# Loads around a layer border taken in contiguous quarters, and w_o loaded one head at a time

## The chip, the cores and the metric

The kernel runs on one core of a Trainium2 chip. The core has TensorE (PE in the profile; its weight loads are listed as PEld), VectorE (DVE), ScalarE (ACT), GpSimd (POOL) and SyncE (SP). In this kernel SP does nothing but issue the loads, which 16 DMA engines carry out. The metric is the time of one execution on the device in microseconds (us). The median of three executions before the change is 650.86 us (650.15 to 652.39).

## The reference

Four tokens (one for each of B = 4 sequences) pass through attention, feed-forward, attention, feed-forward; both attention steps use the same caches and weights, and so do both feed-forward steps.

```python
def _A_ref(x, k_cache, v_cache, wq, wo):      # x [4, 1, 512]; caches [4, 8, 8192, 128], bf16
    q = (x @ wq).reshape(B, Sq, 32, 128).transpose(0, 2, 1, 3)
    k = jnp.repeat(k_cache, 4, axis=1)        # 8 kv heads serve 32 query heads
    v = jnp.repeat(v_cache, 4, axis=1)
    p = softmax(einsum("bhqd,bhkd->bhqk", q, k) * 128 ** -0.5)
    return einsum("bhqk,bhkd->bhqd", p, v).transpose(0, 2, 1, 3).reshape(B, Sq, 4096) @ wo
def _B_ref(x, w_gate, w_up, w_down):          # [512, 1792], [512, 1792], [1792, 512]
    return (silu(x @ w_gate) * (x @ w_up)) @ w_down
x = A_x
for _ in range(2):
    x = x + _A_ref(_layernorm(x), A_k_cache, A_v_cache, A_wq, A_wo)
    x = x + _B_ref(_layernorm(x), B_w_gate, B_w_up, B_w_down)
```

A pair of sequence and kv head has 8192 keys of 128 numbers, 2 MB, and as many values. The 32 pairs make 134 MB a layer.

## The kernel before

**Units and rooms.** One pair of kv head g and sequence b is a *unit* u = 4g + b. Its keys are one load of 2 MB (K u), its values another (V u). SBUF has 8 *slots* of 2 MB for them (`NSLOT`), each spoken of in 8 blocks (`NB`), named `s{slot}.{block}`. Layer 0 takes the units in the order 0 to 31, layer 1 in the order 29, 30, 31, 0 to 28. The keys and values of units 29 to 31 stay in slots 0 to 5 from layer 0 to layer 1 (`NKEEP`), so that layer 1 loads 29 units. At a layer's end w_gate, w_up and w_down lie in slots 6 and 7 (`at_w` gives the blocks of each); w_q, w_o and three quarters of w_up stay in SBUF for good.

**The list of loads.** `items` is one list, in the order in which SP issues: K0, K1, V0, K2, V1, ..., then w_gate, w_up, w_down, and the same for layer 1. `pump` walks it: the slot of the next item is fixed (`home`), and the walk stops where that slot isn't free. `finished` frees a slot once the last scores (K) or products (V) that read it are in the program, and `T.dma` lets SP wait for exactly those. All loads go through SP's one queue in list order. A key or value load is cut by `runs` so that its source is read in rows of 32 KB. The last values of each layer (`split`) are four loads instead, each with 4 KB of every partition. w_o is eight loads of 512 KB (4 KB in a partition), put in pairs behind the 3rd, 5th, 7th and 9th key or value load.

**Around the border.** After the last products of layer 0 come the projection by w_o, layernorm, and `ffn(False)`: w_gate and w_up matmuls, the SiLU on DVE and ACT, w_down in three pieces (`WD`). All of slots 6 and 7 is given free behind the last w_down matmul; K0 and K1 of layer 1 go there. The slot of K29 goes to V0 and that of K30 to K2, by halves (`half`), the first half when four of the eight blocks have been scored. The other slots go on as they are finished.

**The work of a unit.** DVE turns each of the 8 key blocks (`turn`, one 128x512 transpose in place), PE multiplies it (`scores`); then follow maximum, exponentials and the turned probabilities (`max_p` to `total`, kept in `line` and let out between the blocks by `advance`), and `values`: PE multiplies the values, ACT and DVE add up (`own_first`, `own_others`), `add_rows` and `scale_o` write the unit's four heads into `oT`. When four units of a kv head are done, `out_proj` puts `oT` into another order by 16 small matmuls and a copy (`o4`) and multiplies by w_o. PE, DVE and ACT each run their instructions in order. Units 29 to 31 are already turned when layer 1 begins.

**Projection by w_q in layer 1.** The four heads of unit 29's kv head are projected first (`qproj([first])`); the other 28 heads are one lump of 112 matmuls in front of K0's blocks.

**Loops.** `roll` looks for units whose instructions repeat every four units and plays them as a loop on PE, DVE and ACT, each by itself; what lies outside is written out. It starts at the first unit with the longest repeat.

The lines that carry the layer border:

```python
        halves = {("K", 1, unit_order[1][k]): items[ends[0] + 3 + k] for k in range(2)}      # 330
        split = {items[e - 3] for e in ends}                                                 # 328
                      writes=places + ["wg"])                                                # 360
            free.update((NKEEP, NKEEP + 1))                                                  # 731, end of ffn
            pump()
```

Of the kernel before, what the change touches and what calls it, by code (L numbers as in the profile page):

```python
# [8 lines left out]
BF16 = mybir.dt.bfloat16  # L9
# [136 lines left out]
def bass_interleave_layers__gqa_block_cached__swiglu_ffn__decode_kernel(  # L146
# [44 lines left out]
    with ExitStack() as es:  # L191
# [16 lines left out]
        wd_sb = kvf[:, f1:f1 + FO * D].rearrange("p (f n) -> p f n", f=FO)  # L208
        places = [f"s{s}.{q}" for s in range(NKEEP, NSLOT) for q in range(NB)]
        room = lambda a, b: places[(a - f0) // (TB * Dh):(b - 1 - f0) // (TB * Dh) + 1]  # L210
        at_w = {"wg": room(f0, f0 + KT * F) + ["wg"], "wu": room(f0 + KT * F, f1) + ["wu", "wu3"],
                "wd": room(f1, f1 + FO * D)}
        WD = ((0, 6), (6, 12), (12, 14))
        wq_sb = sb("wq_sb", [P, KT, HqDh], BF16)

        wo_sb = sb("wo_sb", [P, G, REP, D], BF16)
        wo_b = wo_sb[:].rearrange("p g e n -> p (g e n)").bitcast(U8)
# [8 lines left out]
        o4 = sb("o4", [P, REP, B], BF16)  # L226
# [40 lines left out]
        sem_h = [[sem(f"sem_h{k}{i}") for i in range(2)] for k in range(2)]  # L267
# [57 lines left out]
        for n, it in ((3, ("wo", 0)), (6, ("wo", 1)), (9, ("wo", 2)), (12, ("wo", 3))):  # L325
            items.insert(n, it)
# [3 lines left out]
        halves = {("K", 1, unit_order[1][k]): items[ends[0] + 3 + k] for k in range(2)}  # L330
# [14 lines left out]
        def runs(src):  # L345

            n = src.shape[0] * src.shape[1] * 2
            return src.rearrange("(r k) n -> r (k n)", r=32 * -(-n // (32 * RUN)))

        def load_weight(name, i=0):  # L350
            if name == "wq":
                T.dma("sp", [(wq_sb[:, i, :], runs(A_wq[i * P:(i + 1) * P, :]))], sem_w["wq"][i], writes=[f"wq{i}"])
            elif name == "wo":
                n = G // 4
                w = REP * Dh
                T.dma("sp", [(wo_sb[:, g, :, :].rearrange("p e n -> p (e n)"), runs(A_wo[g * w:(g + 1) * w, :]))
                             for g in range(i * n, (i + 1) * n)], sem_w["wo"][i], writes=[f"wo{i}"])
# [15 lines left out]
        def pump():  # L373
            while issued[0] < len(items):
# [19 lines left out]
                src = cache[b, g, :, :].rearrange("(p t) d -> p (t d)", p=P)  # L394
                if it in split:
                    w = TT * Dh // NQ
                    n8 = NB // NQ
                    for q in range(NQ):
                        T.dma("sp", [(kv[:, s, q * w:(q + 1) * w], src[:, q * w:(q + 1) * w])], sem_l[q],
                              writes=[f"s{s}.{q * n8 + k}" for k in range(n8)])  # L400
                else:
                    T.dma("sp", [(kv[:, s, :], runs(cache[b, g, :, :]))], sem_s[s], writes=[f"s{s}.{q}" for q in range(NB)])
                issued[0] += 1

        def half(it, i):
            to = halves[it]
            kind, L, u = to
            s = slot_of[it]
            if i == 0:
                assert items[issued[0]] == to  # L410
                slot_of[to] = s
                issued[0] += 1
            w = SL // 2
            src = (A_k_cache if kind == "K" else A_v_cache)[u % B, u // B, :, :].rearrange("(p t) d -> p (t d)", p=P)
            T.dma("sp", [(kv[:, s, i * w:(i + 1) * w], src[:, i * w:(i + 1) * w])], sem_h[unit_order[1].index(it[2])][i],
                  writes=[f"s{s}.{i * NB // 2 + k}" for k in range(NB // 2)])

        def finished(it):
# [5 lines left out]
            elif it in halves:  # L424
                half(it, 1)
                pump()
            else:
                free.add(slot_of[it])
                pump()
# [97 lines left out]
        def keys(L, u):  # L527
            def block(q):
# [9 lines left out]
                if q == NB // 2 - 1 and ("K", L, u) in halves:  # L538
                    half(("K", L, u), 0)
# [4 lines left out]

            for q in range(NB):
                if (L, u, q) not in turned:
                    turn(L, u, q)
# [3 lines left out]
        def values(L, u):  # L551
            g, b = unit_gb(u)
            bk = OBK[turn_of[u]]
            def begin():
# [33 lines left out]
            def add_rows():  # L588
                T.pe(bank(LNB)[:, 0:REP], acc[:], head[:], reads=["acc", "head"], writes=[f"pb{LNB}"],
                     start=True, stop=True)  # L590
                scale_o(LNB)
# [16 lines left out]
            def scale_o(k):  # L608
                T.op("dve", lambda e: e.tensor_tensor(oT[:, g // (G - 1), :, b], bank(k)[:, 0:REP], rl[:, rl_of[u], :],
                                                      ALU.mult),  # L610
                     reads=[f"pb{k}", f"rl{rl_of[u]}"], writes=[f"oT{g // (G - 1)}"])
# [7 lines left out]
            done.add((L, u))  # L619
            if all((L, g * B + k) in done for k in range(B)):  # L620
# [10 lines left out]
        def out_proj(g):  # L631

            pick = ident.rearrange("p (j e) -> p e j", e=REP)
            ob = bank(OUTB)[:, XB:2 * XB].rearrange("p (e b) -> p e b", b=B)
            for c in range(REP):
                for h in range(REP):
                    T.pe(ob[h * QB:(h + 1) * QB, c, :], pick[:, c, :], oT[:, g // (G - 1), h, :],
                         reads=[f"oT{g // (G - 1)}", "ident"], writes=[f"pb{OUTB}"], sig=(h == REP - 1),
                         start=True, stop=True)
            T.op("dve", lambda e: e.tensor_copy(o4[:], ob),  # L640
                 reads=[f"pb{OUTB}"] + [f"wo{i}" for i in range(4)], writes=["o4"])
            for nt in range(KT):
                for c in range(REP):
                    T.pe(bank(OUTB)[:, nt * B:(nt + 1) * B], ((c, nt), wo_at(c * D + nt * P)), o4[:, c, :], at=g,
                         reads=["o4"], writes=[f"pb{OUTB}"], sig=(c == REP - 1), start=(c == 0), stop=(c == REP - 1))
# [212 lines left out]
```

## Time and profile before

| what | value |
|---|---|
| the profiled execution: its time, its span | 651.29 us, 649.3 us |
| busy share of the span: PE, DVE, ACT, POOL | 78%, 69%, 18%, 3% |
| moved by DMA | 274.27 MB, mean 422 GB/s |
| share of 16 DMA engines' span, loads alone | 98.7% |
| mean TensorE clock granted | 0.855 of full |
| issues: K and V whole, w_o, last V in quarters | 118 of 2 MB, 8 of 512 KB, 8 of 512 KB |

The profile is one execution. Its time exceeds its span by 2.0 us, which lies outside the first and the last instruction, and it is 0.43 us longer than the median of the three shown. In the windows below, "DMA share" is the mean busy share of the 16 DMA engines, and it counts a packet where it starts, so that it can pass 1 in a short window. The GB/s beside it are the bytes of those packets. Busy time alone doesn't show what a stage waits for; the time from a load's issue to its landing and the rate of the DMA engines are read together with it.

### The profile page before, as it was taken

How to read it: one execution, taken by the hardware profiler on the slowest of the kernel's cores; microseconds unless marked ns; L12 is line 12 of the kernel's file. 1: busy time of each engine (PE TensorE's matmuls, PEld its weight loads, DVE VectorE, ACT ScalarE, POOL GpSimd, SP SyncE). 2: the span in 40 equal slices, each digit the busy share in tenths (PEclk: the TensorE clock that was granted, in tenths of full speed). 3: DMA queues.
4: the chain of work that ended last, by engine and by line, in shares of the span. 5: the costliest groups of instructions: out<-in, count | busy, mean ns of one | idle time of the engine just before them, and what ended most of it. 6: DMA issues, size and time to landing. Idle time of an engine off the chain costs nothing.

```text
span 649.3 us, 12407 instructions
## 1 busy us (share of the span) xinstructions
PE 505.3 (78%) x4896; PEld 324.7 (50%) x4896; DVE 446.2 (69%) x1079; ACT 116.3 (18%) x391; POOL 19.3 (3%) x73
## 2 busy tenths in 40 slices
PE   1657788878868787886877986898888787886886
PEld 1534454545435454553556654555555454553556
DVE  2556676776866767776762386979797777686683
ACT  0021111211211212221220211213131221121120
POOL 0000000000000000000000000000000000000000
PEclk9998787797987879789795978979897969799795
DMA  8999999999999999999999999999999999999996
GB/s 347 427 431 428 433 429 434 428 440 428 432 436 424 444 426 432 439 424 442 428 416 361 421 408 430 417 439 430 432 438 424 438 430 436 436 424 438 430 415 279
DMA packets 13085, 274.27 MB, mean 422 GB/s; under 512 B 2712, under 2 KB 2720, under 8 KB 3744
## 3 DMA queue, kind: packets, MB, share of 16 engines
q1 hardware_dynamic: 13056, 273.89, 98.7%
q8 instruction: 17, 0.28, 0.2%
q14 instruction: 12, 0.10, 0.0%
HBM read 273.88 MB, written 0.00 MB: 422 GB/s over the span
## 4 chain that ended last, share of the span: by engine, by line
DMA 50%; DVE 24%; PE 21%; issue 3%; SPq 1%; ACT 1%; DVEq 0%; POOL 0%; ACTq 0%; POOLq 0%
DMA kvf<-in_A_k_cache_dram 47%; PE ps L99 21%; DVE kvf L117 15%; DVE acc L117 4%; DMA kvf<-in_B_w_up_dram 3%; DVE one L117 1%; DVE pT L117 1%; SPq L135 1%; DVE m L117 1%; DVE scr L117 1%; ACT pb L117 0%; ACT acc L117 0%; DVE oT L117 0%; DVEq L782 0%; SPq L133 0%
## 5 line engine op out<-in xcount | busy, mean ns | idle before, releaser
L117 DVE STREAM_TRANSPOSE kvf<-kvf 128x512 f32<-128x512 f32 x488 | 322.3, 686 | 68.6 <-DMA kvf<-in_A_k_cache_dram 68.6
L99 PE MATMUL ps<-kvf,zq 128*128 128x256 bf16 x2048 | 332.6, 305 | 21.7 <-DVE kvf L117 16.4
L99 PEld LDWEIGHTS ps<-kvf,zq 128*128 128x128 bf16 x2048 | 202.6, 111 | 92.7 <-DVE kvf L117 40.2
L117 ACT ACTIVATE pb<-m 1x128 f32<-1x128 f32 x64 | 19.7, 308 | 441.1 <-DVE m L117 441.1
L99 PE MATMUL ps<-kvf,pT 128*16 128x512 bf16 x960 | 68.0, 407 | 1.4 <-DVE rl L117 1.4
L117 DVE SCALAR_TENSOR_TENSOR acc<-ps,own,acc 128x128 f32<-128x128 f32 x180 | 63.2, 351 | 6.5 <-ACT acc L117 1.9
L99 PE MATMUL ps<-identf,one 128*1 128x128 f32 x64 | 17.9, 279 | 43.2 <-DVE one L117 43.2
L117 DVE TENSOR_REDUCE one<-ps 128x1 f32<-128x256 f32 x64 | 25.9, 405 | 37.0 <-PE ps L99 36.5
L99 PEld LDWEIGHTS ps<-identf,one 128*1 128x1 f32 x64 | 5.1, 80 | 73.6 <-DVE one L117 67.5
L99 PE MATMUL ps<-head,acc 128*128 128x4 f32 x120 | 24.5, 275 | 21.4 <-DVE acc L117 21.3
L99 PEld LDWEIGHTS ps<-head,acc 128*128 128x128 f32 x120 | 20.5, 214 | 37.0 <-DVE acc L117 36.7
L117 ACT ACTIVATE pb<-ps,one,rstd 128x256 bf16<-128x256 f32 x64 | 36.1, 563 | 2.1
L467 POOL TENSOR_TENSOR zq<-scr,quad 128x64 bf16<-128x64 bf16 x62 | 18.1, 293 | 604.0 <-PE ps L99 564.9
L99 PEld LDWEIGHTS ps<-kvf,pT 128*16 128x16 bf16 x960 | 19.1, 91 | 33.8 <-issue 21.9
L99 PE MATMUL ps<-one,pb 1*128 1x1 f32 x128 | 26.2, 272 | 11.5 <-ACT pb L117 11.2
L99 PEld LDWEIGHTS ps<-one,pb 1*128 1x128 f32 x128 | 20.8, 202 | 28.8 <-ACT pb L117 26.0
L99 PE MATMUL ps<-o,wo_sb 128*128 128x4 bf16 x256 | 26.5, 166 | 9.1 <-DVE o L117 9.1
L117 DVE STREAM_TRANSPOSE pT<-pb 128x256 bf16<-128x256 bf16 x64 | 26.1, 408 | 9.7 <-ACT pb L117 9.7
L99 PEld LDWEIGHTS ps<-rsm,one 128*128 128x128 f32 x128 | 23.9, 232 | 12.2 <-ACT rsm L117 10.4
L99 PEld LDWEIGHTS ps<-o,wo_sb 128*128 (+1 forms) x256 | 22.8, 103 | 12.8 <-issue 9.0
L99 PE MATMUL ps<-rsm,one 128*128 128x4 f32 x128 | 21.7, 240 | 9.0 <-ACT rsm L117 9.0
L117 DVE TENSOR_TENSOR xT<-xT,ps 128x16 f32<-128x16 f32 x21 | 3.6, 172 | 33.1 <-PE ps L99 33.1
(61 smaller groups left out, 197.1 us busy)
## 6 DMA issues: line engine op xcount, KB each, us to landing
kvf<-in_A_k_cache_dram SPq DMA_DIRECT2D x60, 2048.0 KB, 28.8
kvf<-in_A_v_cache_dram SPq DMA_DIRECT2D x58, 2048.0 KB, 31.2
wq_sb<-in_A_wq_dram SPq DMA_DIRECT2D x4, 1024.0 KB, 8.4
wo_sb<-in_A_wo_dram SPq DMA_DIRECT2D x8, 512.0 KB, 37.7
kvf<-in_A_v_cache_dram SPq DMA_DIRECT2D x8, 512.0 KB, 14.7
kvf<-in_B_w_gate_dram SPq DMA_DIRECT2D x8, 448.0 KB, 16.8
kvf<-in_B_w_down_dram SPq DMA_DIRECT2D x14, 256.0 KB, 17.6
kvf<-in_B_w_up_dram SPq DMA_DIRECT2D x5, 448.0 KB, 18.0
```

Of the source, the lines that this page charges most:

```text
L99: return e.matmul(out, lhsT=lhsT if at is None else lhsT(place(at)), rhs=rhs, **kw)
L117: self.tape[engname].append((repr((name, args, kw)), lambda e, _: getattr(e, name)(*args, **kw), left, sig, None))
L135: ins = e.add_instruction(mybir.InstDMACopy(name=self.nc.get_next_instruction_name(), mode="Copy", queue="qSPDynamicHW", ins=e.lower_ap_dm ...
L467: T.op(eng, lambda e: e.tensor_tensor(dst, q4, m4_, ALU.mult), reads=keys_ + ["quad"], writes=["zq"])
```

## The change

- **w_o** is loaded one head at a time: 32 loads of 128 KB in place of 8 of 512 KB. The 128 rows of w_o of a head go one to a partition (1 KB each); the source is read in 16 rows of 8 KB. They stand in threes behind every key or value load from the third on, so that the last two come behind V5. With the head's own rows in the partitions, `out_proj` multiplies `oT` by w_o at once: the 16 ordering matmuls and the copy are gone. The wait for w_o moves from that copy to `scale_o` of the unit that completes a kv head.
- **Slots 6 and 7 given up in parts.** Three quarters of K0 (layer 1) are issued behind the w_gate matmuls, the fourth behind the w_up matmuls; half of K1 behind the first piece of w_down, which is now 8 of 14 blocks, the rest behind the last.
- **Quarters for halves.** V0 and K2 take the slots of K29 and K30 by quarters, after 2, 4, 6 and 8 scored blocks. Every quarter, also of the last values of a layer, is 512 KB that lie together in memory, read in rows of 16 KB and written as 4 KB a partition. The units concerned (the last of each layer; 0, 1, 2 in layer 1) have this order of keys in K and V.
- **Order at the head of layer 1.** DVE turns K0 while K30 is scored and K1 while K31 is scored. V31 is multiplied in front of K0, not behind it, and in front of V31 come the 28 heads of w_q, four at a time. V3's load changes places with K4's.
- **Small things.** `add_rows` uses other columns of its PSUM bank; `roll` takes the latest start among those with the same number of turns.

```diff
+        WD = ((0, 8), (8, 12), (12, 14))
...
-                "wd": room(f1, f1 + FO * D)}
-        WD = ((0, 6), (6, 12), (12, 14))
+                **{f"wd{j}": room(f1 + a * D, f1 + b * D) + [f"wd{j}"] for j, (a, b) in enumerate(WD)}}
...
-        for n, it in ((3, ("wo", 0)), (6, ("wo", 1)), (9, ("wo", 2)), (12, ("wo", 3))):
-            items.insert(n, it)
+        for h in range(Hq):
+            items.insert(3 + h // 3 * 4 + h % 3, ("wo", h))
+        i, j = (items.index((k, 1, unit_order[1][2 * NRES + n])) for k, n in (("K", 1), ("V", 0)))
+        items[i], items[j] = items[j], items[i]
...
+        heirs = {("K", 1, unit_order[1][k]): items[ends[0] + 3 + k] for k in range(2)}
+        fours = {(L, unit_order[L][-1]) for L in range(2)} | {(1, u) for u in unit_order[1][NRES:2 * NRES]}
...
+                T.dma("sp", [(wo_sb[:, i, :], runs(A_wo[i * Dh:(i + 1) * Dh, :], 16))], sem_w["wo"][i // G],
+                      writes=[f"wo{i}"])
...
+        def part(it, s, a, b, sem_):
+            kind, L, u = it
+            assert (L, u) in fours
+            n = NB // NQ
+            w, m = n * TB * Dh, S // NQ
+            src = (A_k_cache if kind == "K" else A_v_cache)[u % B, u // B, :, :]
+            T.dma("sp", [(kv[:, s, q * w:(q + 1) * w], runs(src[q * m:(q + 1) * m, :])) for q in range(a // n, b // n)],
+                  sem_, writes=[f"s{s}.{k}" for k in range(a, b)])
+
+        def place(it, s):
+            assert items[issued[0]] == it
+            slot_of[it] = s
+            issued[0] += 1
+
+        def quarter(it, i):
+            to = heirs[it]
             if i == 0:
+                place(to, slot_of[it])
+            n = NB // NQ
+            part(to, slot_of[it], i * n, (i + 1) * n, sem_h[unit_order[1].index(it[2])][i])
...
-                if q == NB // 2 - 1 and ("K", L, u) in halves:
-                    half(("K", L, u), 0)
+                if ("K", L, u) in heirs and (q + 1) % (NB // NQ) == 0 and q < NB - 1:
+                    quarter(("K", L, u), q // (NB // NQ))
...
+            i = unit_order[L].index(u)
+            ahead = unit_order[1][i + 2] if L == 1 and i in (1, 2) else u
             for q in range(NB):
-                if (L, u, q) not in turned:
-                    turn(L, u, q)
+                if (L, ahead, q) not in turned:
+                    turn(L, ahead, q)
...
-                     reads=[f"pb{k}", f"rl{rl_of[u]}"], writes=[f"oT{g // (G - 1)}"])
+                     reads=[f"pb{k}", f"rl{rl_of[u]}"] + [f"wo{h}" for h in range(Hq) if whole],
+                     writes=[f"oT{g // (G - 1)}"])
...
         def out_proj(g):
-            for c in range(REP):
-                for h in range(REP):
-                    T.pe(ob[h * QB:(h + 1) * QB, c, :], pick[:, c, :], oT[:, g // (G - 1), h, :],
...
+                    T.pe(bank(OUTB)[:, nt * B:(nt + 1) * B], ((c, nt), wo_at(c * D + nt * P)), oT[:, k, c, :], at=g,
+                         reads=[f"oT{k}"], writes=[f"pb{OUTB}"], sig=(c == REP - 1), start=(c == 0), stop=(c == REP - 1))
...
+            ks = items[ends[0] + 1:ends[0] + 3]
+            w6 = KT * F // (TB * Dh) // 2 * 2
             for (w_sb, wname, bk) in (([wg_sb[:, k, :] for k in range(KT)], "wg", gb), (wu_sb, "wu", ub)):
...
+                if not last:
+                    if bk == gb:
+                        place(ks[0], NKEEP)
+                        part(ks[0], NKEEP, 0, w6, sem_p[0])
+                    else:
+                        part(ks[0], NKEEP, w6, NB, sem_p[1])
...
-            free.update((NKEEP, NKEEP + 1))
-            pump()
+                if j == 0 and not last:
+                    place(ks[1], NKEEP + 1)
+                    part(ks[1], NKEEP + 1, 0, NB // 2, sem_p[2])
+            if not last:
+                part(ks[1], NKEEP + 1, NB // 2, NB, sem_p[3])
...
-                n = max(run, key=run.get)
+                n = max(run, key=lambda n: (run[n] // CYCLE, n))
...
+            if L == 1:
+                todo.remove(("V", 1, unit_order[1][2]))
+                todo.insert(todo.index(("K", 1, 0)), ("V", 1, unit_order[1][2]))
+            for i, (kind, _, u) in enumerate(todo):
+                if L == 1 and (kind, u) == ("V", unit_order[1][2]):
+                    for k in rest_q[0]:
+                        blocks.append((0.5, lambda k=k: qmul([k])))
+                    blocks.append((0.5, lambda gs=rest_q[0]: qrows(gs)))
```

## The prediction

> **What bounds the kernel now.** I read the page's slices and queues first, then stages by windows, then the loads in order of time.
>
> ```profile
> GB/s 347 427 431 428 433 429 434 428 440 428 432 436 424 444 426 432 439 424 442 428 416 361 421 408 430 417 439 430 432 438 424 438 430 436 436 424 438 430 415 279
> q1 hardware_dynamic: 13056, 273.89, 98.7%
> ```
>
> No engine is busy for more than 78% of the span, but the loads fill 98.7% of the 16 DMA engines. The rate is flat near 430 GB/s except in the first slice, the last, and around slice 21 (341 to 357 us), where layer 0 gives way to layer 1. The windows show these places:
>
> ```profile
> 60.00:320.00 260.00, 205.35 (x1650) 127.15 (x1654) 184.89 (x434) 46.03 (x156) 7.61 (x26) 0.83 1.00 432
> 328.00:331.00 3.00, 2.53 (x22) 1.82 (x21) 3.00 (x6) 1.12 (x4) 0.00 (x0) 1.00 0.80 330
> 346.00:360.00 14.00, 10.24 (x140) 7.71 (x136) 2.48 (x13) 0.56 (x2) 0.29 (x1) 0.55 0.88 343
> 360.00:380.00 20.00, 18.18 (x256) 13.37 (x257) 9.44 (x26) 5.07 (x17) 0.58 (x2) 0.89 1.04 442
> 380.00:388.00 8.00, 7.35 (x60) 4.75 (x61) 6.64 (x15) 1.77 (x6) 0.29 (x1) 0.84 0.88 342
> 388.00:510.00 122.00, 102.16 (x901) 63.14 (x898) 100.81 (x237) 24.79 (x84) 4.39 (x15) 0.92 1.01 433
> 625.00:630.00 5.00, 4.53 (x42) 2.98 (x43) 4.39 (x11) 1.52 (x5) 0.00 (x0) 1.00 0.90 383
> ```
>
> The last two columns are DMA share and GB/s. Layer 0 runs at 432 with share 1.00. Against that the border loses 14 x (432-343)/432 = 2.9 us in 346:360 and 8 x (432-342)/432 = 1.7 us in 380:388, and 360:380 gives 0.5 back: **4.1 us** net. From 388 on the rate is whole again, although the chain of waits runs through DVE there: the queue still holds loads, so a DVE gap in that stretch costs nothing. A load that starts earlier at the border therefore ends the kernel earlier by as much. The two stretches at 328 and 625 are where the quarters with 4 KB packets begin; they lose 3 x 102/432 = 0.7 and 5 x 49/432 = 0.6 us.
>
> Why the queue runs dry is read from SP's issues in order of time:
>
> ```profile
> 326.77 9.42 SPq L135 DMA_DIRECT2D kvf<-in_B_w_down_dram  x7
> 347.99 2.38 SPq L135 DMA_DIRECT2D kvf<-in_A_k_cache_dram  x2
> 356.84 3.07 SPq L133 DMA_DIRECT2D kvf<-in_A_v_cache_dram  x2
> 362.13 2.85 SPq L133 DMA_DIRECT2D kvf<-in_A_k_cache_dram  x2
> 371.69 0.47 SPq L135 DMA_DIRECT2D kvf<-in_A_v_cache_dram  x1
> 383.63 0.47 SPq L135 DMA_DIRECT2D kvf<-in_A_k_cache_dram  x1
> 384.62 0.47 SPq L135 DMA_DIRECT2D kvf<-in_A_v_cache_dram  x1
> ```
>
> After w_down (issued by 336.2) nothing follows until 347.99, when the w_up matmuls are done; w_down has landed by 349.0, and the first packets of K0 start at 349. Between V2 (371.69) and K4 (383.63) there are 12 us without an issue; V2 lands at 387.1.
>
> **The change, part by part.**
>
> *Slots 6 and 7 in parts.* The w_gate matmuls end at 343.8, so three quarters of K0 (1.57 MB, 3.6 us at 432) are issued at about 343.9 and stand behind w_down, whose packets end near 348: busy to 351.6. The fourth quarter (w_up matmuls done, 347.9) brings 1.2 us, to 352.8. K1's halves (after w_down's first piece, about 349.1, and its last, 349.9) bring 2.4 us each, to 357.7. Seven loads more on SP at 0.6 us each are hidden, since SP waits between them. An issue takes some 1 to 2 us to its first packet (347.99 to 349), so none is late.
>
> *Quarters for V0 and K2.* Each is 1.2 us of transfer, and PE scores two blocks in about 1.3 us. V0's come from 354.3 on, before 357.7, and fill to 362.5. K2's come from about 360.9 on, at the pace of PE: first packet at 362.7, and the last, issued at 364.6, ends near 368. I leave 0.5 us idle here. In 346:360 the gain is thus most of 2.9.
>
> *The order at the head of layer 1.* DVE is busy for 2.5 us in 346:360 and has room. It turns 16 blocks of 0.65 us = 10.4 us ahead of K0. The first three stand before K29's maximum, K0's first part has landed by about 353; the other 13 (8.5 us) share 358.5 to 370.5 with 5 us of softmax and sums, 13.5 us in 12, so K31 ends some 1 to 1.5 us later and with it K3 and V2. SP's queue behind K3 is V2, V3, K4, in this order. V31 needs K31's softmax, some 3.5 us from maximum to turned probabilities; the 112 w_q matmuls (2.94 us) lie in front of it and cover most of that. V31 then ends near 378 and V3 is issued there, not at 384.62; K0, already turned, is pure PE, 8 x 0.65 = 5.2 us, so K4 goes at about 384. The queue has V2 to 383.5, V3 to 388.5, K4 to 393.4. The hole of 1.7 us closes. `add_rows` shares its bank with the w_q matmuls, so PE may wait once or twice for DVE, under 1 us each, covered by V2.
>
> Sum of the border: 4.1 less 0.5 = **-3.6 us**.
>
> *16 KB rows for 4 KB rows.* The quarters now have a quarter of the packets. w_o before, in 16 KB rows, shows no loss (24 to 36 us: 433). The 0.7 and 0.6 us could go; the bounds are 0 and -1.3. I take **-0.9**, nearer the w_o rows. Eight units' loads in rows of 16 rather than 32 KB and more semaphore writes: 2 x 611 for 1213 ns a packet and 9 ns a write, together **+0.3**.
>
> *w_o by heads.* The nearest row is w_down: 8 KB packets in 2 KB pieces, 414 GB/s (344 to 346) against 432. 4.19 MB then take 10.1 instead of 9.7 us; with 384 more semaphore writes of 9 ns on 16 engines **+0.6**. The bound above is the output's 1 KB packets at 48 ns: 8 x 48 = 384 for 309 ns, 32 packets an engine, +2.4 +0.2 = +2.6. Below it is 0; nothing in fewer bytes a piece can gain. SP issues 32 instead of 8, 0.6 us each, 14.4 us more, but the engines are then 20 us and more behind SP: hidden. Were they not, see the third rival.
>
> *The wait for w_o in `scale_o`.* The first one that needs all of w_o ran at 78.87. w_o's last head now stands behind V5, which was issued at 52.52 and landed at 88.85. DVE stops for about 10.7 us, and all turns behind it, so PE and SP's next issue, K9 (85.80), wait to about 96.5. Loads issued by then last to 108 us: hidden with 11 us to spare. Price if that cover were gone: what exceeds it.
>
> *`out_proj`.* 16 times 16 small matmuls and a copy go. They matter only ahead of the two feed-forwards: 0.70 us each (pick matmuls 637.33, w_o matmuls 638.03). At the end w_gate lands at 640.03, and PE began it at 640.12: w_gate is late next, so I count 0. In layer 0 it lets K0's first part go 0.7 us sooner, behind w_down anyway: 0. w_down as 8+4+2: its last 256 KB gate as before, 0.
>
> **Sum:** -3.6 -0.9 +0.3 +0.6 = -3.6 us on 651.29, 647.7; the median lies 0.43 under the profiled execution, so **647.3 us**.
>
> **A rule against it.** The row: w_down's 256 KB loads follow each other at 414 GB/s, so transfers of that size lose 4% here. The Trainium skill, "DMA: Bandwidth & Descriptors", section "Bandwidth", says to batch loads to 1 MiB or more and lists 0.95 us for 64 KB and 6.15 us for 1 MB; between these I estimate 1.3 us for 128 KB and 3.4 for 512 KB, hence 32 x 1.3 less 8 x 3.4, some +14 us. These are times of one load by itself; the trace, with a full queue, doesn't agree.
>
> **The rivals.**
>
> *Second: only the first hole closes.* DVE's turns ahead hold K31's softmax longer than 1.5 us, K3, V2 and V3 come late, and 380:388 stays. For it: 13.5 us of DVE in 12. Against: V3 no longer waits for K0. The gain is 2.9 less 0.5 and no packet gain: 650.86 -2.4 +0.9 = 649.4. The 1 KB rows at their upper bound end at 649.3 as well.
>
> *Third, the other side: each w_o load costs the queue its issue time.* If an engine gets its next small load no sooner than SP's 0.60 us, w_o takes 32 x 0.60 = 19.2 instead of 9.7 us, +9.5 in place of +0.6: 656.2. It turns the gain into a loss from 0.43 us a load on (without w_o the sum is -4.2, and 32 x 0.43 is 4.2 over 9.7). Against it: w_gate's and w_up's loads land about 1.1 us apart for 448 KB, at full rate, and w_o's stand behind 2 MB loads.
>
> *Fourth: a loop entry falls where the queue is thin.*
>
> ```profile
> 395.36 0.69 DVE L117 STREAM_TRANSPOSE kvf<-kvf 128x512 f32<-128x512 f32 x1
> 398.42 0.26 ACT L117 ACTIVATE one<-ps,rstd 128x1 f32<-128x1 f32 x1 [5.40 <-issue]
> ```
>
> ACT enters layer 1's loop at 392.5 and stands for 5.4 us; in layer 0 it is 6.5 us at its entry. Now the loads outstanding reach to 407, so nothing is lost. The new `roll` takes a later start, about two units on, with 7 us outstanding by my times. If the start stays and the queue is 3 to 4 us thinner, up to 5.4 us come back: 652.7. The Trainium skill, "Runtime: NRT & Kernel Launch", section "Instruction fetch mechanics", says a taken branch out of the fetched pages stalls for the fetch; the trace agrees, 5.40 us.
>
> **Chances.** Forecast 0.58, with its own range 645.2 to 648.9. Second with the 1 KB rows 0.19; third 0.08; fourth 0.08; something dearer on DVE or PE in layer 1 that I don't see, 0.07. A measurement here can't tell less than about 0.3%, 2 us, from no change: 648.9 to 652.8 is "same". Faster: 0.58 and a third of the second, 0.65. Same: the rest of the second and half of the fourth, 0.18. Slower: the rest, 0.17. The range 645.0 to 653.0 takes in all gains with no cost (-5.4: 645.5) and the fourth, and leaves out about 0.18.
>
> **What would show it.** First, K issues near 344 and 348 and no window below 400 GB/s between 346 and 360; then V3 before K4 with V3 near 378, and 380:388 near 430. DVE idle for some 10 us before an `oT` row near 79 us, waiting for w_o, with DMA at 430 in 80 to 110. 8 KB packets of w_o near 315 ns. The last w_down landing some 3.5 us earlier, with the same 4 us to the end. The prediction is wrong if DMA idles in the first 110 us, if the queue runs dry again between 365 and 415, or if the w_o stage falls well under 414 GB/s.

## The result: 2.4% slower, and where the time went

The changed kernel takes 666.85 us (median of 4 runs, 664.07 to 667.36) against 650.6 us before (with a fourth execution; the three shown ahead gave 650.86): the ratio is 1.0236, with a 95% interval of 1.0201 to 1.0270. I had forecast 647.3 us and a range up to 653.0, so the prediction was wrong in its sign. The profiled execution took 667.36 us, with a span of 665.6. One of the four executions of e2 below ran in a slower state (697.75 us) and is left out of its median.

The slices and the queues of the changed kernel come first, as they did for before:

```profile
GB/s 365 411 343 323 316 321 396 436 430 431 433 431 437 427 433 433 435 428 435 425 428 419 382 401 435 432 428 435 429 435 431 433 433 433 433 433 433 421 429 287
q1 hardware_dynamic: 13408, 273.90, 99.0%
```

The bytes are the same. The share of the DMA engines did not fall (99.0% against 98.7%), yet five slices, from 33 to 116 us (a slice is 16.6 us), carry 316 to 396 GB/s where before had 430. Nothing as long shows in the rest. The windows of the changed kernel give the size (the last two columns are DMA share and GB/s; the border comes later than before, so its windows are shifted):

```profile
26.00:108.00 82.00, 40.72 (x374) 26.10 (x372) 33.94 (x76) 8.61 (x29) 1.47 (x5) 0.66 1.01 336
108.00:340.00 232.00, 191.05 (x1482) 118.03 (x1482) 174.73 (x404) 44.31 (x150) 7.34 (x25) 0.85 1.00 433
356.00:372.00 16.00, 8.75 (x212) 7.84 (x213) 5.17 (x25) 0.81 (x3) 0.00 (x0) 0.50 1.02 423
372.00:380.00 8.00, 7.50 (x48) 5.28 (x46) 3.41 (x7) 0.87 (x3) 0.29 (x1) 0.71 0.92 354
380.00:388.00 8.00, 7.35 (x69) 5.14 (x69) 7.64 (x18) 2.99 (x10) 0.29 (x1) 1.00 1.02 367
```

Before, the first of these windows had this line:

```profile
26.00:108.00 82.00, 59.04 (x552) 37.80 (x550) 53.49 (x123) 13.91 (x47) 2.34 (x8) 0.84 1.00 429
```

The stretch in which w_o is loaded loses 82 x (433 - 336) / 433 = **18.4 us**. The share there is 1.01: the engines do not wait for work, each packet takes longer. This is the last of the signs that I had named, a w_o stage well under 414 GB/s. From the trace's records of single packets, mean time of one:

```
                            w_o packet         32 KB packet of K and V
before, 26 to 112 us        -                  1217 ns
changed, 26 to 112 us       432 ns (8 KB)      1511 ns, up to 2340
e7 (below), 26 to 108 us    311 ns (8 KB)      1217 ns
```

The units' packets beside w_o's are slowed too, and they are most of the loss: 764 packets of 1511 instead of 1217 ns are 14 us on 16 engines, w_o's own 512 packets are 4. The border, from which most of my gain was to come, gained little: from the landing of layer 0's last values to that of the pair V3 and K4, 61.5 us became 60.1.

A list of the chain that ended last would mislead here. In the changed kernel it reads "DMA 48%; PE 18%; DVE 17%; SPq 13%", against 1% for SP's queue before, as if the issues were the bound. They take part because SP is held: with 14 to 16 loads issued and not yet landed, 20 issues before 110 us took 1.3 to 4.4 us instead of 0.6, as these lines of SP's issues show (start, duration; the last is three issues).

```profile
8.68 1.88 SPq L135 DMA_DIRECT2D wo_sb<-in_A_wo_dram  x3
13.90 3.90 SPq L135 DMA_DIRECT2D kvf<-in_A_k_cache_dram  x1
17.84 11.27 SPq L135 DMA_DIRECT2D wo_sb<-in_A_wo_dram  x3
```

### The profile page after: what moved, and what is told of

Its sections match the earlier page's. It is cut to its first block, busy times and chain, and to the rows that moved or that the text cites. A ratio compares the mean times of both kernels' runs of the same rounds, so it can differ in the third digit from the quotient of the medians.

```text
span 665.6 us, 11935 instructions
## 1 busy us (share of the span) xinstructions
PE 505.0 (76%) x4640; PEld 324.5 (49%) x4640; DVE 446.1 (67%) x1063; ACT 116.6 (18%) x391; POOL 19.3 (3%) x73
## 2 busy tenths in 40 slices
DMA packets 13438, 274.28 MB, mean 412 GB/s; under 512 B 3448, under 2 KB 3456, under 8 KB 3456
## 4 chain that ended last, share of the span: by engine, by line
DMA 48%; PE 18%; DVE 17%; SPq 13%; issue 3%; ACT 1%; DVEq 0%; POOL 0%; ACTq 0%; POOLq 0%
DMA kvf<-in_A_k_cache_dram 38%; PE ps L99 18%; SPq L135 13%; DVE kvf L117 11%; DMA wo_sb<-in_A_wo_dram 5%; DMA kvf<-in_B_w_gate_dram 3%; DVE acc L117 3%; DMA kvf<-in_B_w_down_dram 2%; DVE one L117 1%; DVE pT L117 1%; DVE m L117 1%; DVE scr L117 0%; ACT pb L117 0%; DVE oT L117 0%; DVEq L799 0%
## 5 line engine op out<-in xcount | busy, mean ns | idle before, releaser
L99 PE MATMUL ps<-kvf,zq 128*128 128x256 bf16 x2048 | 337.1, 309 | 23.9 <-DVE kvf L117 15.0
L99 PEld LDWEIGHTS ps<-kvf,zq 128*128 128x128 bf16 x2048 | 206.1, 113 | 96.0 <-DVE kvf L117 37.1
L99 PE MATMUL ps<-oT,wo_sb 128*128 128x4 bf16 x256 | 26.4, 165 | 23.5 <-DVE oT L117 23.5
L99 PEld LDWEIGHTS ps<-oT,wo_sb 128*128 (+1 forms) x256 | 22.3, 101 | 30.6 <-issue 27.0
L117 DVE TENSOR_TENSOR oT<-ps,rl 128x4 bf16<-128x4 f32 x64 | 8.6, 134 | 27.0 <-DMA wo_sb<-in_A_wo_dram 19.0
```

The lines of the kernel that those rows point to most:

```text
L99: return e.matmul(out, lhsT=lhsT if at is None else lhsT(place(at)), rhs=rhs, **kw)
L117: self.tape[engname].append((repr((name, args, kw)), lambda e, _: getattr(e, name)(*args, **kw), left, sig, None))
```

## The experiments

Two groups of kernels were used. One starts from the changed kernel and alters how w_o is loaded. The other ("border alone") has everything of the change but w_o, which is loaded and used as before, and alters one thing in that. All ratios are against the kernel before on the same chip (medians of 650.6 to 650.9 us). "Packets" is the number of source rows of one w_o load over the 16 engines; a row is one packet in the trace. The kernels here differ in speed, so the rate from 26 to 108 us covers different amounts of work; it serves as a sign of the loss.

| run | start; w_o loads | packets an engine and load | us | ratio, interval | GB/s, 26:108 |
|---|---|---|---|---|---|
| changed | 32 of 128 KB | 1 of 8 KB | 666.85 | 1.0236 [1.0201, 1.0270] | 336 |
| e1 | border alone; 8 of 512 KB | 2 of 16 KB | 648.51 | 0.9968 [0.9957, 0.9978] | 432 |
| e2 | changed; source rows far apart | 1 of 8 KB | 667.32 | 1.0226 [1.0176, 1.0276] | 336 |
| e3 | changed; 4 KB pieces | 1 of 8 KB | 664.8 | 1.0230 [1.0197, 1.0264] | 342 |
| e4 | changed; all 32 in a row | 1 of 8 KB | 653.28 | 1.0041 [1.0023, 1.0058] | 398 |
| e8 | changed; shorter queue | 1 of 8 KB | 665.68 | 1.0226 [1.0188, 1.0263] | 348 |
| e14 | changed; in groups of six | 1 of 8 KB | 663.88 | 1.0210 [1.0189, 1.0231] | 366 |
| e9 | changed; 32 rows | 2 of 4 KB | 648.37 | 0.9970 [0.9958, 0.9981] | 427 |
| e5 | border alone; 32 of 128 KB | 1 of 8 KB | 656.51 | 1.0090 [1.0063, 1.0117] | 383 |
| e13 | e5, neighbouring partitions | 1 of 8 KB | 663.81 | 1.0195 [1.0174, 1.0216] | 363 |
| e6 | border alone; 16 of 256 KB | 2 of 8 KB | 648.39 | 0.9959 [0.9944, 0.9974] | 430 |
| e10 | e6, 16 rows | 1 of 16 KB | 658.36 | 1.0127 [1.0102, 1.0153] | 374 |
| e7 | border alone; 8 of 512 KB | 4 of 8 KB | 648.19 | 0.9954 [0.9937, 0.9971] | 432 |
| e11 | border alone; quarters strided | 2 of 16 KB | 647.98 | 0.9955 [0.9941, 0.9968] | 430 |
| e12 | border alone; old order | 2 of 16 KB | 649.91 | 0.9985 [0.9975, 0.9995] | 432 |
| e15 | border alone; w_down 1 packet | 2 of 16 KB | 654.13 | 1.0053 [1.0034, 1.0071] | 431 |

### Which part loses the time: e1

Only w_o's loads and `out_proj` are put back.

```diff
-        for h in range(Hq):
-            items.insert(3 + h // 3 * 4 + h % 3, ("wo", h))
+        for n, it in ((3, ("wo", 0)), (6, ("wo", 1)), (9, ("wo", 2)), (12, ("wo", 3))):
+            items.insert(n, it)
...
-            k = g // (G - 1)
+            pick = ident.rearrange("p (j e) -> p e j", e=REP)
...
```

> The changed kernel with w_o loaded and used as before (8 loads of 512 KB, the ordering matmuls and the copy), all the border's changes kept. Both theories below put the loss on w_o's loads: the stretch 26 to 108 us of the changed kernel moved 336 GB/s where layer 0 otherwise moves 433, which is 82 x 97/433 = 18.4 us. From the last values of layer 0 to the first two loads behind the border the changed kernel is 1.3 us quicker than the one before (60.1 for 61.5 us). So about 649 us here, 648 to 650.5, with 430 GB/s or more in 26 to 108. If the border's changes cost time themselves, over 652.

Measured: 648.51 us. The windows of this kernel, of the w_o stretch and of the border:

```profile
26.00:108.00 82.00, 60.35 (x548) 38.37 (x545) 54.05 (x124) 13.92 (x47) 2.35 (x8) 0.81 1.01 432
346.00:360.00 14.00, 10.30 (x143) 8.26 (x144) 5.91 (x20) 0.58 (x3) 0.29 (x1) 0.66 0.99 404
360.00:380.00 20.00, 18.65 (x260) 13.01 (x259) 13.61 (x34) 5.41 (x18) 0.59 (x2) 0.83 1.00 412
380.00:388.00 8.00, 7.50 (x73) 5.63 (x75) 2.49 (x8) 1.52 (x5) 0.56 (x2) 1.00 1.06 451
```

So the whole loss lies in w_o's part (e9 below narrows it to the loads), and the border by itself is a gain of 2.4 us: 650.87 to 648.51. The two holes, 343 and 342 GB/s before, stand at 404 and 451, but the stretch between them, 442 before, is now 412.

### Where w_o's loads come from and what they are cut into: e2, e3

Theory A put the loss down to the source (all 16 engines read one 128 KB stretch); theory B to the 1 KB pieces in which a row is written. e2 takes the 16 rows of a load 256 KB apart; e3 writes 4 KB pieces to 32 partitions, four apart. Both bring rows of w_o to places where they don't belong.

```diff
-                T.dma("sp", [(wo_sb[:, i, :], runs(A_wo[i * Dh:(i + 1) * Dh, :], 16))], sem_w["wo"][i // G],
+                T.dma("sp", [(wo_sb[:, i, :], A_wo.rearrange("(r h k) n -> h r (k n)", h=Hq, k=8)[i])], sem_w["wo"][i // G],
```

```diff
-                T.dma("sp", [(wo_sb[:, i, :], runs(A_wo[i * Dh:(i + 1) * Dh, :], 16))], sem_w["wo"][i // G],
+                T.dma("sp", [(wo_sb[:].rearrange("p (g e) n -> p g (e n)", e=REP)[i % REP::REP, i // REP, :],
+                             runs(A_wo[i * Dh:(i + 1) * Dh, :], 16))], sem_w["wo"][i // G],
```

> The changed kernel; each w_o load still takes 16 rows of 8 KB and writes them as 1 KB a partition, but the rows lie 256 KB apart and not together in 128 KB (so the heads' rows lie in other places than the projection reads, and the output is not the reference's). Theory A, the source: 16 DMA engines reading one stretch of 128 KB get in each other's way; then the stretch 26 to 108 us recovers to 420 GB/s or more and the time falls to about 649. Theory B, the pieces of 1 KB in SBUF, and theory C, small loads standing between large ones: no change, 664 to 668 us.

> The changed kernel; each w_o load still takes the same 128 KB in 16 rows of 8 KB at the same place in the list, but writes 4 KB to each of 32 partitions, four apart, instead of 1 KB to each of 128 (so the projection reads other rows than it needs, and the output is not the reference's). Theory B, the 1 KB pieces: the loss goes, about 649 us. Theories A (source) and C (small loads between large ones): 664 to 668 us.

Measured: 667.32 and 664.8 us. Neither gives the time back, so both theories fall as the main cause; the 2 us of e3 are within what the runs of one kernel differ by.

### All in a row, or behind a shorter queue: e4, e8

e4 puts the 32 loads behind V0 without units in between. e8 leaves them in threes, but before each three SP waits until the third-last unit load has landed, so that its queue isn't full (at most 8 others are then outstanding).

```diff
-            items.insert(3 + h // 3 * 4 + h % 3, ("wo", h))
+            items.insert(3 + h, ("wo", h))
```

```diff
+                    if it[0] == "wo" and it[1] % 3 == 0:
+                        far = [x for x in items[:n] if x[0] in "KV"][-3]
+                        T.wait_res("sp", reads=[f"s{slot_of[far]}.0"])
                     load_weight(*it)
```

> The changed kernel with all 32 w_o loads in one row behind V0 instead of in threes between the key and value loads. Theory C, the mixing: only the two ends of that row still mix, so 4.19 MB take about 10 to 12 us and the time falls to 649 to 652 us. Theory B (pieces) and A (source): every w_o packet stays as slow as it was, 432 instead of 315 ns, and hinders the loads around it as before, 660 to 668 us.

> The changed kernel, w_o by heads in threes as it is, but SP waits in front of each three until the third last key or value load has landed, so that no more than about 12 loads are outstanding and SP is never held at an issue. Theory E: the loss goes, 649 to 652 us, with 420 GB/s or more in 26 to 108. Theories D and F: 664 to 668.

Measured: 653.28 and 665.68 us. e8 says that the held issues are a consequence and no cause. e4 loses 4.9 us against e9 below. The other 13.6 of the changed kernel's 18.5 us are back, though each load still gives an engine one packet: much of what theory C (small loads between large ones) expected came true, so where the loads stand matters beside what they are. A good part of what is left has another cause. The windows of e4:

```profile
26.00:36.00 10.00, 8.25 (x148) 6.31 (x144) 6.04 (x12) 1.52 (x5) 0.29 (x1) 0.83 0.97 354
36.00:46.00 10.00, 0.85 (x7) 0.53 (x6) 0.00 (x0) 0.00 (x0) 0.29 (x1) 0.74 0.81 239
```

In the second window the share is 0.81: the loads go at SP's pace here, one issue of 128 KB in 0.63 us with three or four outstanding, which is some 210 GB/s. This is my third rival, and this is the only run in which it shows. The w_o packets were longer as well, 359 ns in the mean in the first window and 455 in the second, against 311 in e7.

### Size of a load, or packets for an engine: e5, e6, e7

These cut the 512 KB loads of the border alone into four of 128 KB (16 rows of 8 KB) and into two of 256 KB (32 rows of 8 KB), or leave them whole and read them in rows of 8 KB. The diffs are against e1. In e5 and e6 the rows land in other partitions than the reference wants.

```diff
-                T.dma("sp", [(wo_sb[:, g, :, :].rearrange("p e n -> p (e n)"), runs(A_wo[g * w:(g + 1) * w, :]))
-                             for g in range(i * n, (i + 1) * n)], sem_w["wo"][i], writes=[f"wo{i}"])
+                T.dma("sp", [(wo_sb[j::4, g, :, :].rearrange("p e n -> p (e n)"),
+                              runs(A_wo[g * w + j * (w // 4):g * w + (j + 1) * (w // 4), :], 16))
+                             for g in range(i * n, (i + 1) * n) for j in range(4)], sem_w["wo"][i], writes=[f"wo{i}"])
```

e6 has, in the same place,

```diff
+                T.dma("sp", [(wo_sb[j::2, g, :, :].rearrange("p e n -> p (e n)"),
+                              runs(A_wo[g * w + j * (w // 2):g * w + (j + 1) * (w // 2), :], 32))
+                             for g in range(i * n, (i + 1) * n) for j in range(2)], sem_w["wo"][i], writes=[f"wo{i}"])
```

and e7 amounts to `runs(A_wo[g * w:(g + 1) * w, :], 64)` in the first of the lines taken out.

> The kernel of e1 (648.5 us) with w_o at the same four places, the same bytes at each and 4 KB in a partition, but each 512 KB load cut into four loads of 128 KB (16 rows of 8 KB, 32 partitions four apart; rows land in other partitions than the projection expects, so the output is not the reference's). Theory D, the count of loads: each load that gives an engine a single packet costs the engines about 0.57 us (18.4 us over 32 loads), so 648.5 + 18 = 666. Theory E, the queue is full: SP was held for 2 to 4 us at an issue with 16 loads outstanding, and the engines are fed badly as long as that lasts; 32 loads in eights fill the queue as well, but only until 60 us, so 655 to 666. Theory F, the number of places where small loads stand between large ones: 4 places for 10.7, so 648.5 + 7 = 655.

> The same with each 512 KB load cut into two of 256 KB (32 rows of 8 KB, two packets an engine). Theory D: 16 loads, half the cost or, if only single packets cost, none: 648.5 to 657. Theory E: 4 loads a place with 7 key or value loads reach 16 outstanding only shortly: 649 to 652. Theory F: 655.

> The same with the loads left at 512 KB but read in rows of 8 KB and not 16 (64 packets instead of 32 a load). If the packet's size of 8 KB between packets of 32 KB is what costs, 655 to 666; theories D and E: 648.5 to 649.5, as e1.

Measured: 656.51, 648.39 and 648.19 us. The 8 KB packet costs nothing (e7), and 256 KB loads cost nothing (e6). 128 KB loads cost 8 us. Between e5 and e6 more than one thing differs, though: the bytes of a load, the partitions it fills (32 that lie four apart, or 64 that lie two apart), and the packets it gives each engine, one or two.

### One number: e9 and e10

e9 is the changed kernel with the least number of source rows of a w_o load set to 32. The loads stay at 128 KB, at the same places in the list, to the same partitions, with as many semaphore writes; each engine gets two packets of 4 KB instead of one of 8 KB. e10 is the reverse: e6's 256 KB loads, to the same partitions, in 16 rows of 16 KB (its diff is against e6).

```diff
-                T.dma("sp", [(wo_sb[:, i, :], runs(A_wo[i * Dh:(i + 1) * Dh, :], 16))], sem_w["wo"][i // G],
+                T.dma("sp", [(wo_sb[:, i, :], runs(A_wo[i * Dh:(i + 1) * Dh, :], 32))], sem_w["wo"][i // G],
```

```diff
-                              runs(A_wo[g * w + j * (w // 2):g * w + (j + 1) * (w // 2), :], 32))
+                              runs(A_wo[g * w + j * (w // 2):g * w + (j + 1) * (w // 2), :], 16))
```

> The changed kernel with one number changed: a head of w_o is read in 32 rows of 4 KB, not 16 rows of 8 KB, so that each load of 128 KB gives each of the 16 engines two packets. Load count, sizes, places and 1 KB pieces stay. Theory G, only the single packet an engine costs: about 648 us, as e1, with 420 GB/s or more in 26 to 108. Theory H, a load's size of 128 KB (its 0.3 us of transfer) costs: 664 to 668 as before.

> The kernel of e6 (256 KB loads, 648.4 us) with each load read in 16 rows of 16 KB instead of 32 of 8 KB: again a single packet an engine, with twice the bytes of the changed kernel's (rows land in other partitions than the projection expects, so the output is not the reference's). Theory G: the loss is back, 652 to 657 us (e5 with single packets of 8 KB at these four places: 656.5). Theory H: 648.4 as e6.

Measured: 648.37 and 658.36 us. The size of the load is not it (theory H); the loss comes and goes with the number of source rows, 16 or 32, as theory G has it (a single packet for each engine). The DMA view of the changed kernel from 26 to 108 us,

```profile
DMA packets 1918, 27.59 MB, mean 336 GB/s; under 512 B 688, under 2 KB 688, under 8 KB 688
q1 hardware_dynamic: 1911, 27.50, 100.7%
```

and the same view of e9:

```profile
DMA packets 2722, 35.03 MB, mean 427 GB/s; under 512 B 752, under 2 KB 752, under 8 KB 1776
q1 hardware_dynamic: 2714, 34.93, 100.4%
```

More packets and smaller ones, in engines that are equally full, and 27% more bytes. In e9 a w_o packet takes 163 ns for 4 KB and a unit's packet 1218 ns for 32 KB, in the mean from 26 to 112 us, against 432 (for 8 KB) and 1511. SP is held in e9 as in the changed kernel (20 issues over 1.2 us before 110 us, 50 us in all; there 20 and 62), at no loss: that, too, says that the held issues are no cause. e9 also shows the wait for w_o in `scale_o` undisturbed (start, duration, idle time before):

```profile
88.39 0.17 DVE L117 TENSOR_TENSOR oT<-ps,rl 128x4 bf16<-128x4 f32 x1 [12.86 <-DMA wo_sb<-in_A_wo_dram]
```

### Partitions, places, another weight: e13, e14, e15

The first diff is against e5. e13 is e5 with each load's 32 partitions next to one another, e14 the changed kernel with w_o in groups of six, e15 the border alone with w_down's 14 loads (256 KB) in 16 rows of 16 KB.

```diff
-                T.dma("sp", [(wo_sb[j::4, g, :, :].rearrange("p e n -> p (e n)"),
+                T.dma("sp", [(wo_sb[j * 32:(j + 1) * 32, g, :, :].rearrange("p e n -> p (e n)"),
```

```diff
-            items.insert(3 + h // 3 * 4 + h % 3, ("wo", h))
+            items.insert(3 + h // 6 * 7 + h % 6, ("wo", h))
```

```diff
-                                  runs(B_w_down[f * P:(f + 2) * P, :])) for f in range(a, b, 2)], sem_w["wd"][j],
+                                  runs(B_w_down[f * P:(f + 2) * P, :], 16)) for f in range(a, b, 2)], sem_w["wd"][j],
```

> The border's change alone, with every 512 KB load of w_o cut into four of 128 KB in 16 rows of 8 KB, as in the run that measured 656.5 us, but each load now fills 32 partitions that lie next to one another instead of 32 that lie four apart (values and layout are the reference's in this one). Theory G (what costs is a load that hands each of the 16 engines a single packet): 655 to 658 us, w_o packets again near 380 ns for 16 of them a load, and 32 KB packets behind them above 1350 ns. Rival P (what costs is which partitions the 16 engines write at the same time: with rows that lie apart each engine's write is scattered): 648.5 us, as with the whole loads, and 430 GB/s from 26 to 108 us.

> The changed kernel with its 32 loads of w_o (128 KB, one packet an engine) in groups of six between units instead of groups of three: five full places and a part of one in place of eleven. Theory per place (each change from units to w_o and back costs about 18.4 / 10.7 = 1.7 us, however many w_o loads stand there): 5.3 places x 1.7 = 9.1 us over the 648.4 of two packets an engine, so 657.5 us. Theory per load (each such load costs 18.4 / 32 = 0.57 us): 666.8 us, as changed. In between, each w_o load of a longer group also costs its issue on SP, 0.6 us for 0.3 us of data, so up to 2 us more on the first.

> The border's change alone, with the 14 loads of w_down (256 KB each, seven in a row a layer) read as 16 rows of 16 KB, one packet an engine, instead of 32 rows of 8 KB. Theory G per place: two places of 1.7 us, 651.9 us, less if the second one, at the end of layer 1, has DMA time to spare. Theory G per load (0.57 us each): up to 14 x 0.57 = 8.0 us, 656.5 us. Rival (single packets cost only in turn with units' 32 KB packets in a full queue of early layer 0): 648.5 us, as with 32 rows.

Measured: 663.81, 663.88 and 654.13 us.

- e13: rival P falls, since the scattered write was not what cost. But the partitions do matter to the size: neighbours cost 15.3 us over e1, four apart only 8.0, where I had expected the same.
- e14: the price per place (657.5) falls. Half the places cost 15.5 us over e9 instead of 18.5; that is nearer to a price per load, which e4 doesn't fit either (4.9 us for all 32).
- e15: the loss is not in w_o's stage alone, nor only a matter between 8 KB and 32 KB packets. w_down's seven loads follow one another in a full queue, and the window in which they and K0 run falls from this line of e1

```profile
340.00:350.00 10.00, 5.66 (x170) 5.30 (x170) 2.60 (x13) 0.81 (x3) 0.00 (x0) 0.50 1.02 422
```

to this one of e15, with no less share:

```profile
340.00:350.00 10.00, 4.28 (x116) 4.08 (x116) 2.17 (x11) 0.81 (x3) 0.00 (x0) 0.50 1.04 295
```

The loads' 16 KB packets took 906 ns in the mean from 340 to 356 us, against 618 in e1. The profiled execution of e15 was the slowest of its six (656.71 us, 652.60 to 656.71), so the median lost less than these lines show.

### The border's own parts: e11, e12

e11 reads the quarters as before, 4 KB of every partition, and whole loads elsewhere; e12 takes back the order at the head of layer 1 (K0 and K1 turned ahead, V31 in front of K0, w_q by fours, V3 before K4).

```diff
-                elif (L, u) in fours:
-                    part(it, s, 0, NB, sem_s[s])
...
-            src = (A_k_cache if kind == "K" else A_v_cache)[u % B, u // B, :, :]
-            T.dma("sp", [(kv[:, s, q * w:(q + 1) * w], runs(src[q * m:(q + 1) * m, :])) for q in range(a // n, b // n)],
+            src = (A_k_cache if kind == "K" else A_v_cache)[u % B, u // B, :, :].rearrange("(p t) d -> p (t d)", p=P)
+            T.dma("sp", [(kv[:, s, q * w:(q + 1) * w], src[:, q * w:(q + 1) * w]) for q in range(a // n, b // n)],
```

```diff
-        items[i], items[j] = items[j], items[i]
...
-            ahead = unit_order[1][i + 2] if L == 1 and i in (1, 2) else u
+            ahead = u
...
-                todo.remove(("V", 1, unit_order[1][2]))
-                todo.insert(todo.index(("K", 1, 0)), ("V", 1, unit_order[1][2]))
...
```

> The kernel of e1 with every quarter read as in the kernel before, 4 KB out of each partition's 16 KB, in packets of 4 KB, and the units loaded whole in 32 KB rows where no quarter is wanted; what the quarters wait for is as in the change. If the contiguous quarters are worth what I took (-0.9, between 0 and -1.3), 649.0 to 650 against 648.5; if the border's gain is all in when the loads are issued, 648.5.

> The kernel of e1 with the head of layer 1 in the order before: K0 and K1 turned when they are scored, V31 behind K0, the 28 heads of w_q in one lump ahead of K0, K4 loaded ahead of V3. Slots 6 and 7 and those of K29 and K30 are still given up by quarters. If the order closes the hole behind V2 as I reckoned (1.7 us), this comes to 650.2 and shows a window near 345 GB/s at the place of 380 to 388 us; if the earlier loads alone make the gain, 648.5.

Measured: 647.98 and 649.91 us. Reading the quarters as contiguous rows brings nothing that can be told. The order is worth 649.91 - 648.51 = 1.4 us, and without it the second hole stays, as the windows of e12 show:

```profile
346.00:360.00 14.00, 11.15 (x136) 8.54 (x137) 2.34 (x13) 0.56 (x2) 0.29 (x1) 0.60 1.02 414
360.00:380.00 20.00, 18.18 (x252) 13.13 (x251) 10.64 (x29) 5.08 (x17) 0.59 (x2) 0.86 1.00 408
380.00:388.00 8.00, 7.34 (x65) 4.83 (x64) 6.72 (x16) 1.77 (x6) 0.29 (x1) 0.93 0.90 340
```

### What the runs leave open

They show when it happens: in every kernel here whose loads of w_o or w_down have 16 rows, one packet for each of the 16 engines, those packets lengthen. w_o's 8 KB packets took 359 ns (e4, first window) to 538 (e13) instead of 311, and the engines were kept full, but for e4. The packets around them lengthen in most places too.

They don't show what inside the queue does it, nor a rule for the size. Per load it is 0.58 us (changed), 0.51 (e3), 0.48 (e14, e13), 0.25 (e5), 0.62 (e10), 0.40 (e15) and 0.15 (e4, SP's pace included), each from the difference to e1 or e9. Part of the spread goes with the places: loads that fill 32 partitions four apart cost 16.4 us in threes between units (e3) and 8.0 in eights (e5), and the changed kernel's own loads 18.5 in threes, 15.5 in sixes and 4.9 in one row. Why was not tried.

For every such load the trace has 16 packets of 4 bytes, the semaphore writes, with 16 rows and with 32 (3448 in all in the changed kernel and in e9), which fits a share for each of the 16 engines. Which rows an engine gets of a load of 32 is not in the trace, so it may also be that an engine then writes other partitions than with 16 rows; no run here separates that from the count.

## Why the prediction was wrong, step by step

**The step that failed: "w_o by heads", +0.6 us, bounded by 0 and +2.6.** Against e1, which lacks this part, it measured 666.85 - 648.51 = 18.3 us. With 32 rows (e9) it measures nothing that can be told, so the whole of it comes with the 16 rows: 666.85 - 648.37 = 18.5 us. I priced a packet by its bytes and its pieces, from w_down's row: 8 KB in 2 KB pieces at 414 GB/s. e9, e7 and e6 agree with that, as far as it goes: neither 128 KB loads nor 4 or 8 KB packets cost anything measurable. What I didn't count was packets per load and engine. 16 rows for 16 engines is one; w_down's 32 rows are two, and no key, value or weight load of before gives an engine fewer than two. The row that I called the nearest was on the other side of the step, and so my upper bound, which took only the cost of smaller pieces, was no bound.

**The rule that I weighed.** The Trainium skill, "DMA: Bandwidth & Descriptors", section "Bandwidth", speaks against small loads, and my estimate from it was +14 us. I set it aside because w_down's row had a full queue. The sign and nearly the size came out as in that estimate, but that is luck as far as these runs show: in e9 the loads are just as small and the stretch runs at 427 GB/s. The page's table is also for loads that GpSimd issues, not SP.

**The third rival, on the slower side,** was each load's issue time, 656.2 us. The place was right, the mechanism was not: the DMA share of 1.01 in that stretch excludes it, and it shows only in e4. None of my rivals had the mechanism that decided; the outcome "slower" had a chance of 0.17 (my own terms add up to 0.19, and those of "same" to 0.17).

**The border, -3.6 us.** e1 holds all of it, together with my -0.9 for contiguous rows and +0.3 for the smaller ones: -4.2 predicted, -2.4 measured.

- *The order*: 1.7 predicted for the hole in 380:388, 1.4 measured (e12). V3 was to go near 378 and K4 near 384; in e1 the issues are

```profile
370.49 8.06 SPq L135 DMA_DIRECT2D kvf<-in_A_v_cache_dram  x5
382.59 5.55 SPq L135 DMA_DIRECT2D kvf<-in_A_k_cache_dram  x2
```

  where the last of the five, at 378.08, is V3. DVE's 13.5 us in 12 did not hold it up, so the second rival falls.
- *Rooms and quarters*: 2.9 less 0.5 for idle time, less the 0.5 that 360:380 had given back, is 1.9 predicted; 650.83 - 649.91 = 0.9 measured (e12, which also holds the quarters' rows). K0's first issue came at 342.38 in e1, before the 343.9 that I gave it. But the stretch 360:380 carries 412 instead of 442, at a share of 1.00: the loss is not idle time, as I had it. The 16 KB packets of the quarters are longer there, 0.71 us in the mean from 360 to 364 in e1 and in e9, against 0.62 for w_o's before. It is not their size alone: in e11, where the quarters come in packets of 4 KB, these take 179 ns in 360:380 against 160 in the kernel before, and the stretch runs at 397. The cause stays open.
- *16 KB rows for 4 KB rows*, -0.9, with +0.3 for the units in smaller rows: nothing measurable together (e11). The stretch 325:335 runs at 414 with them (e1) and at 413 without.
- In the changed kernel itself the border gained only 1.4 us (61.5 to 60.1, as above), with 354 and 367 GB/s between 372 and 388; in e1 the same stretch takes 59.2 us and in e9 59.6.

**What held.** The wait for w_o in `scale_o` is hidden: in e9 DVE stands for 12.9 us (10.7 predicted), K9 goes at 94.4 (96.5 predicted) and the loads outstanding last to 107.9. Even in the changed kernel, with 19.0 us of wait, the rate from 108 us on is 433. The fourth rival's stall at ACT's loop entry is there and hidden. It comes one unit later (in e9 at the sixth softmax of layer 1, 403.34, before at the fifth, 398.42), where I had taken about two. In the changed kernel:

```profile
422.74 0.26 ACT L117 ACTIVATE one<-ps,rstd 128x1 f32<-128x1 f32 x1 [5.60 <-issue]
```

The tail after the pair V3 and K4 takes 251.3 us against 251.9, so that `out_proj` and w_down in 8, 4 and 2 blocks are worth nothing measurable, as counted.

**Better than both kernels:** the change with w_o's loads in 32 rows (e9, 648.37 us, 0.9970 [0.9958, 0.9981]), or without the w_o part (e1, e7, e11; 647.98 to 648.51). These four can't be told apart. e6 is as fast, but brings rows of w_o to partitions where they don't belong.

## What to carry to other kernels

When a load is cut smaller, count its source rows against the 16 DMA engines before its bytes: here loads of 128 KB with two packets an engine left the stage at 427 GB/s, and loads of 128 or 256 KB with a single packet, between other loads, took 11 to 30% of the rate (383 of 432 GB/s in e5, 295 of 422 in e15's window), their neighbours' packets included. A rate that falls at a DMA share of 1.0 means longer packets, not missing work, so look at the packets' own durations and don't go after issues and waits, even where the chain names them. And a row of the trace bounds an unseen cost only if it lies on the same side of every count that changes, not just near in bytes.

## What the runs showed of the hardware that I had not expected

- A load of 16 rows with others queued behind it slows itself and most of the loads around it: 8 KB packets from 311 (e7) to 432 ns and 32 KB packets from 1217 to 1511 ns in the mean (changed kernel), 16 KB packets from 618 (e1) to 906 ns (e15). With 32 rows and the same bytes it is 163 ns for 4 KB and 1218 ns for 32 KB (e9). The short queue of e8, with at most 8 others outstanding, did not help (665.68 us).
- For such loads the partitions matter: the same 32 loads cost 8.0 us where each fills 32 partitions four apart (e5) and 15.3 us where they lie side by side (e13).
- SP's issues were held, at 1.3 to 4.4 us instead of 0.6, from 14 to 16 outstanding loads on in the changed kernel and in e9. That is no fixed count of loads: in e5 and e13, whose w_o loads write 32 pieces of 4 KB and not 128 of 1 KB, 27 to 31 stood outstanding when an issue was held. What the limit counts was not tried.
